# First modulation sums in four column groups, V's weights split on VectorE, the first unit packed in two halves

## The chip, the cores and the metric

The kernel runs on one core of a Trainium2 chip. The metric is the time of one execution on the device in microseconds (us), the median of several runs. Engines are named as the profile names them: PE is TensorE (its matmuls; PEld is its weight loads), DVE is VectorE, ACT is ScalarE, POOL is GpSimd, and SP is the engine that issues nearly all DMAs here; SPq stands for its queue.

## The reference

One transformer block with modulated norms, sequence 2048, width 576, 32 heads of 18, a causal window of 256 keys, and a mixer with an MLP of width 4608. All inputs are float32.

```
mod = (silu(c) @ w_mod).reshape(1, 6, 1, 576)
sa, ca, ga, sb, cb, gb = mod[:, 0], ..., mod[:, 5]
h = layernorm(x) * (1 + ca) + sa
x = x + ga * (windowed_attention(h @ wqkv) @ wo)
h = layernorm(x) * (1 + cb) + sb
x1 = h + shift(gelu(layernorm(h) @ w1)) @ w2
x = x + gb * (x1 + gelu(layernorm(x1) @ w3) @ w4)
```

The condition c is one row of 576 values, and w_mod is 576 x 3456. The change touches how `sa` and `ca` (the first 1152 columns of `w_mod`) are computed, and how the first quarter of the attention gets its operands.

## The kernel before

**Stages.** Phase A computes the norm, q, k and v, the attention and the output projection; phases B and C compute the mixer and the MLP. Sequence rows come in 16 tiles of 128; a group g is four tiles (512 rows). A unit is four heads of one group, so a group has 8 units, and attention has 32. The change is in phase A, in the work ahead of and around the first units of group 0.

**Precision.** Most products split each operand into a high half (a cast to fp32r) and a low half (the rest after subtraction), and sum three products: high by high, high by low, low by high. With 4 full row chunks and one of 64 rows this makes 14 matmuls for each item. So every weight and activation is first cast (mostly on ACT or POOL) and then subtracted (on DVE or POOL).

**Order.** Each piece of work is a small function with a hand-written time in units of an attention unit; `play` runs the pieces in the order of these times. That order is the order of instructions on each engine, and each engine works through its own list in order. Times below zero lie ahead of the first unit. So a piece that waits holds up all that stands behind it on its engine, SP's DMA issues included.

**The first stretch, in that order.** `warm` keeps PE busy with empty matmuls. `c_load` (L237) zeroes a tile, runs one Exp on ACT from that tile (which loads ACT's function table) and loads c. `wm_load` (L254) loads five row chunks of the needed part of `w_mod`. `cond` (L245) computes silu(c) and copies it to 128 equal columns for each chunk (`silub`). The four row tiles of group 0 are loaded and normalised (`x_norm`). `mod_sum(k)` (L269) multiplies a chunk of `w_mod` by the 128 equal columns, so that every partition of four PSUM banks holds the sums; `mod_col(j)` (L279) then picks out the diagonal of a 128x128 piece with the identity matrix as a mask, one DVE reduction for each piece of `sa` and `ca`, ten in all. `x_tr` (L357) transposes the normalised rows on PE, and then makes h on ACT with `sa` and `ca` (L373), its high half on POOL (L376) and its low half on DVE (L380), for five chunks.

**q, k and v of group 0.** `qk_item(g, c)` is one of nine blocks of 128 q or k features; blocks 0, 4 and 5 come first, as unit 0 needs rows of these. Its result is copied by ACT (L412), cast and subtracted by POOL (L416, L420), and stored by SP to arrays in device memory (`qd`, `kd`, L428 to L434). `v_item` is one half of a tile of V; V's weights are loaded by `v_load` (L322) and split by `v_split` (L326): cast on ACT (L330), subtracted on POOL (L334). `w_load` and `w_split` do the same for the blocks of q and k weights (L299, L306, L311). `kinds` and the table in the `v_item` loop name the PSUM bank each item uses: "mm" and "av" are single banks, "sc" is three and "st" two.

**The attention unit.** `pack(u)` (L457) reads the unit's q and k rows back from device memory into tiles with three copies (high, low and high of q; high, high and low of k), six transfers for Q (L467) and six for K (L469), in turn, all on SP. `scores(u)` multiplies them (L483), and a DVE reduction (L490) takes each row's maximum; the maxima go back into the Q tile by a DMA, and `attend(u)` computes the exponentials and the product with V (L530, L539, L549, L560). L560 writes the four heads of a unit to four groups of 32 output partitions.

**Tables that set the order.** `wt` (L664) has the times of the weight loads, `first` (L665) the times of the q/k items of group 0, `vt` (L689) those of the V items. Row buffers with the tag "r" are six; the tiles of x, `silub` and V's raw weights take them in turn. The tag "oT" has one buffer, not used yet this early.

## Time and profile before

| | |
|---|---|
| median of 3 runs | 1737.53 us (1730.81 to 1741.58) |
| profiled execution | 1739.16 us, span of the instructions 1737.4 us |
| mean granted PE clock | 0.989 |
| PE / PEld busy | 96% / 83% of the span |
| DVE / POOL / ACT busy | 67% / 47% / 40% |
| HBM traffic | 168.86 MB read, 111.78 MB written |

All times inside the execution count from the start of the span. A row of the timeline has the start, the time from the first to the last of the merged instructions, the engine, the line, the operation, what it writes and reads, the shape and the count; in brackets stands the idle time of the engine before it and what ended that. A row of a table by stretches has the stretch, its length, the busy time of PE, PEld, DVE, ACT and POOL with the number of instructions, the granted PE clock (1.00 is full), the busy share of the DMA engines and the GB/s. A row of a group has the busy time in us, the mean of one in ns, and the idle time before it with its releasers. PE's busy time counts each matmul from start to end, and matmuls overlap, so its start-to-start distance is read from rows with a count.

### The profile page before, as it was taken

What the parts mean: (1) busy time and instruction counts of PE and PEld (TensorE: products, weight loads), DVE (VectorE), ACT (ScalarE), POOL (GpSimd) and SP (SyncE); (2) the same over time, 40 slices, a digit from 0 to 9 for tenths busy, and PEclk for the clock granted to TensorE, in tenths of its full rate; (3) what the DMA queues carried; (4) which work ended last, traced back from release to release, by engine and by line L of the source; (5) the groups of instructions that cost most, each with busy time, mean ns of one, the idle gap of its engine ahead of it and who ended that gap; (6) DMA issues with size and microseconds to landing.
All of it is one profiled execution on the core that took longest, in us unless ns stands there. A gap on an engine that the chain in (4) does not pass through costs nothing.

```text
span 1737.4 us, 30750 instructions
## 1 busy us (share of the span) xinstructions
PE 1665.6 (96%) x11100; PEld 1439.1 (83%) x11100; DVE 1172.6 (67%) x2543; ACT 700.9 (40%) x1310; POOL 812.6 (47%) x799
## 2 busy tenths in 40 slices
PE   7899999999999889999999999999999999999997
PEld 5777777877777777788989999999998999999997
DVE  3465566665567574777778888888876666666667
ACT  3254464554455555443243444343422222222221
POOL 6433141332225453044178888888864333332335
PEclk9999999999999899999999999999999999999999
DMA  5735544534557563653456555556665554445441
GB/s 167 201 122 150 150 128 134 155 107 125 137 154 197 154 195 110 203 158 103 162 182 219 210 201 187 186 206 221 216 217 166 168 165 146 143 137 168 156 150 68
DMA packets 161279, 283.33 MB, mean 163 GB/s; under 512 B 38500, under 2 KB 77412, under 8 KB 161128
## 3 DMA queue, kind: packets, MB, share of 16 engines
q1 hardware_dynamic: 158184, 275.54, 50.8%
q10 hardware_dynamic: 2944, 5.83, 1.2%
q8 instruction: 88, 1.44, 0.4%
q14 instruction: 63, 0.52, 0.1%
HBM read 168.86 MB, written 111.78 MB: 162 GB/s over the span
## 4 chain that ended last, share of the span: by engine, by line
PE 81%; DMA 6%; DVE 5%; POOL 3%; ACT 2%; issue 1%; SPq 1%; ACTq 0%; POOLq 0%; DVEq 0%
PE pall L1283 26%; PE pall L1329 22%; PE pall L391 8%; PE pall L560 4%; PE pall L530 4%; PE pall L483 4%; PE pall L1017 3%; PE pall L539 3%; PE pall L1068 2%; PE pall L786 2%; DVE pall L490 1%; DMA Q<-ms 1%; DMA wm<-in_w_mod_dram 1%; PE pall L276 1%; PE pall L571 1%
## 5 line engine op out<-in xcount | busy, mean ns | idle before, releaser
L1283 PE MATMUL pall<-LNT,W 128*128 128x512 f32 x2016 | 498.5, 390 | 1.9 <-ACT g L1287 1.9
L1329 PEld LDWEIGHTS pall<-W,G 128*128 128x128 f32 x3036 | 430.0, 189 | 25.9 <-DVE G L1249 4.3
L1329 PE MATMUL pall<-W,G 128*128 128x288 f32 x3036 | 443.4, 295 | 5.7 <-DVE G L1249 3.6
L1283 PEld LDWEIGHTS pall<-LNT,W 128*128 128x128 f32 x2016 | 365.7, 188 | 61.6 <-ACT g L1287 2.2
L490 DVE CUSTOM_DVE_ANT_0 pall<-pall,mask 128x384 f32<-128x384 f32 (+2 forms) x512 | 271.0, 543 | 209.2 <-PE pall L483 205.8
L1338 DVE TENSOR_TENSOR accA<-pall,accA 128x576 f32<-128x576 f32 x336 | 254.2, 757 | 127.3 <-PE pall L1329 115.2
L1254 POOL TENSOR_TENSOR g<-g,g 128x512 f32<-128x512 f32 x140 | 183.9, 1314 | 293.5 <-DVE G L1249 151.1
L549 ACT ACTIVATE P<-pall 128x512 f32<-128x512 f32 (+2 forms) x384 | 215.3, 570 | 166.0 <-PE pall L539 149.5
L1246 ACT CAST G<-g 128x512 fp32r<-128x512 f32 x249 | 151.0, 620 | 282.0 <-POOL g L1254 280.3
L1249 DVE TENSOR_TENSOR G<-g,G 128x512 fp32r<-128x512 f32 x249 | 241.5, 971 | 4.1 <-ACT G L1246 4.1
L483 PE MATMUL pall<-K,Q 108*128 108x384 f32 (+2 forms) x512 | 188.4, 379 | 13.5 <-DMA xnd<-s4rows 4.0
L530 PE MATMUL pall<-Q,K 110*128 110x384 f32 (+1 forms) x704 | 156.8, 297 | 16.7 <-ACT P L549 12.4
L1287 ACT ACTIVATE g<-pall 128x512 f32<-128x512 f32 x144 | 85.8, 596 | 201.7 <-PE pall L1283 192.1
L391 PE MATMUL pall<-hT,Wc 128*128 128x512 f32 x504 | 159.2, 415 | 3.4 <-ACT V L454 1.9
L1338 DVE TENSOR_TENSOR accB<-pall,accB 128x576 f32<-128x576 f32 x134 | 101.4, 757 | 89.8 <-PE pall L1329 87.7
L530 PEld LDWEIGHTS pall<-Q,K 110*128 110x128 f32 x704 | 125.1, 192 | 39.1 <-ACT P L549 20.9
L416 POOL CAST qe<-qe 128x512 fp32r<-128x512 f32 x36 | 22.6, 627 | 240.8 <-ACT qe L412 230.4
L539 PE MATMUL pall<-maskb,identb 128*128 128x256 bf16 (+1 forms) x640 | 121.4, 255 | 0.0
L483 PEld LDWEIGHTS pall<-K,Q 108*128 108x128 f32 x512 | 97.5, 195 | 21.4 <-issue 8.8
L391 PEld LDWEIGHTS pall<-hT,Wc 128*128 128x128 f32 x504 | 86.1, 192 | 17.3 <-issue 3.9
L391 PE MATMUL pall<-Wv,hT 128*128 128x288 f32 x448 | 85.0, 313 | 3.5 <-POOL Wv L334 2.4
L560 PE MATMUL pall<-P,V 128*32 128x384 f32 (+2 forms) x1408 | 86.9, 394 | 0.0
(651 smaller groups left out, 2076.9 us busy)
## 6 DMA issues: line engine op xcount, KB each, us to landing
w4d<-W SPq DMA_DIRECT2D x55, 576.0 KB
W<-w4d SPq DMA_DIRECT2D x55, 576.0 KB
w3d<-W SPq DMA_DIRECT2D x36, 640.0 KB
W<-w3d SPq DMA_DIRECT2D x36, 640.0 KB
K<-k0d SPq DMA_DIRECT2D x96, 108.0 KB
r<-in_B_w_dram SPq DMA_DIRECT2D x36, 288.0 KB
Q<-q0d SPq DMA_DIRECT2D x128, 72.0 KB
K<-k1d SPq DMA_DIRECT2D x48, 108.0 KB
```

What stands on the lines that cost most here:

```text
L391: nc.tensor.matmul(pm, pl()[i][0], pl()[i][1], start=(i == 0), stop=(i == 13))
L483: nc.tensor.matmul(sc[:, lo:], q[0:2 * R3, h, i * P:(i + 1) * P], k[0:2 * R3, h // 2, i * P + lo:(i + 3) * P], start=True, stop=True)
L490: nc.vector.tensor_tensor_reduce(out=sc[:, lo:], in0=sc[:, lo:], in1=mask[:, lo:], scale=1.0, scalar=-3e38, op0=ALU.add, op1=ALU.max, accu ...
L530: nc.tensor.matmul(x[:, p0 * P:(p0 + w) * P], k[0:2 * R3 + 2, h // 2, (kb + 2) * P:(kb + 3) * P], q[0:2 * R3 + 2, h, q0 * P:(q0 + w) * P], ...
L539: nc.tensor.matmul(x[:, p0 * P:(p0 + w) * P], self.identb, m, start=False, stop=(n == len(ms) - 1))
L549: nc.scalar.activation(pt[:, c0:c1, h % 2, :], x[:, c0 * P:c1 * P].rearrange("p (a b) -> p a b", b=P), AF.Exp, scale=SCALE)
L560: nc.tensor.matmul(abox[0][32 * h:32 * h + 32, q0 * P:(q0 + w) * P], v[:, hh * VA:hh * VA + 32], Pt[b, h // 2][:, p0:p0 + w, h % 2, :], st ...
L1249: nc.vector.tensor_tensor(out=sp[m][:, 1], in0=src(), in1=sp[m][:, 0].bitcast(F32), op=sub)
L1254: nc.gpsimd.tensor_tensor(out=g[o] if o in g else gt(o), in0=g[a], in1=g[b], op=op)
L1283: nc.tensor.matmul(box["p"], box["l"][i][1], box["l"][i][0], start=(i == 0), stop=(i == 13))
L1329: nc.tensor.matmul(po, a, b, start=(n == 0), stop=(n == len(seq) - 1))
L1338: nc.vector.tensor_tensor(out=acc2[m, i], in0=po, in1=acc2[m, i], op=ALU.add)
```

## The change

Three things are done, and some times and bank names move with them.

**Modulation.** The equal columns are 32, not 128. The sums of a chunk are four matmuls with 320 columns each: shift and scale, columns 0 to 319 and 256 to 575. Each writes 32 output partitions of one bank. After the last chunk DVE copies the 128x320 result to SBUF (`mod_row`), PE transposes it in three pieces (`mod_tr`), and DVE picks one column of each group of 32 and adds 0 or 1 (`mod_col`, four instructions in place of ten reductions with their reads). The copy and `silub` share the buffer with the tag "oT", so `silub` no longer takes a row buffer. The table-loading Exp reads a constant, and only the unused corner of c's tile is zeroed, so that c's loads wait for neither.

**Splits.** The low halves of V's weights and of q/k block 0's weights go from POOL to DVE. V's splits get other times.

**Pack.** Unit 0's pack becomes two pieces: the Q transfers at -7.6, ahead of the load for block 6 and of block 5's stores, and the K transfers at -7.3 as before.

Besides: the weight load for block 1 goes behind V's loads; block 6's item is completed ahead of unit 0's scores (-1.08 to -0.98); several items take the other of the two banks; the last transpose of x takes a bank of "st".

```diff
-                nc.vector.memset(ct, 0.0)
-                nc.scalar.activation(silu[:, 0:1], ct[:, 0:1], AF.Exp)
+                nc.vector.memset(ct[TAIL:, KC:KC + 1], 0.0)
+                nc.scalar.activation(silu[:, 0:1], self.mhalf, AF.Exp)
...
-                wm["s"] = gp.tile([P, KC + 1, P], F32, tag="r", name="silub", bufs=6)
-                nc.vector.tensor_copy(wm["s"], silu.unsqueeze(2).to_broadcast([P, KC + 1, P]))
+                box = gp.tile([P, 480], F32, tag="oT", name="silub", bufs=1)
+                wm["s"], wm["r"] = box[:, 0:160].rearrange("p (k m) -> p k m", m=32), box[:, 160:480]
+                nc.vector.tensor_copy(wm["s"], silu.unsqueeze(2).to_broadcast([P, KC + 1, 32]))
...
             def mod_sum(k):
                 def f():
                     kk = P if k < KC else TAIL
-                    for v in range(2):
-                        for i, (c0, c1) in enumerate(half):
-                            if k == 0:
-                                wm[v, i] = ps([P, 512], ("sc", "st")[v], f"pms{v}{i}")
-                            nc.tensor.matmul(wm[v, i][:, 0:c1 - c0], wm["s"][:kk, k, :], wm["t"][:kk, k, v * D + c0:v * D + c1], start=(k == 0), stop=(k == KC))
+                    if k == 0:
+                        wm["p"] = ps([P, 320], "sc", "pms")
+                    for q, (v, c0) in enumerate((v, c0) for v in range(2) for c0 in (0, 2 * P)):
+                        nc.tensor.matmul(wm["p"][32 * q:32 * q + 32, :], wm["s"][:kk, k, :], wm["t"][:kk, k, v * D + c0:v * D + c0 + 320], start=(k == 0), stop=(k == KC))
                 return f
 
-            def mod_col(j):
...
-                        nc.vector.tensor_tensor_reduce(out=pm, in0=pm, in1=self.ident[:n, :n], scale=1.0, scalar=float(v), op0=ALU.mult, op1=ALU.add, accum_out=dst[:n, j:j + 1])
-                return f
+            def mod_row():
+                nc.vector.tensor_copy(wm["r"], wm["p"])
+
+            def mod_tr():
+                wm["q"] = ps([P, 3, P], "sc", "pmt")
+                for j in range(3):
+                    n = P if j < 2 else TAIL
+                    nc.tensor.transpose(wm["q"][:n, j, :], wm["r"][:, j * P:j * P + n], self.ident)
+
+            def mod_col():
+                for v, dst in ((0, sa), (1, ca)):
+                    pq = wm["q"].rearrange("p j (v i r) -> p v i j r", v=2, r=32)[:, v, :, :, 0]
+                    nc.vector.tensor_scalar(dst[:, 0:KC].rearrange("p (i j) -> p i j", j=2), pq[:, :, 0:2], float(v), None, op0=ALU.add)
+                    nc.vector.tensor_scalar(dst[:TAIL, KC:KC + 1], pq[:TAIL, 1, 2:3], float(v), None, op0=ALU.add)
...
-                    nc.gpsimd.tensor_tensor(out=w[:, l, :], in0=Wv["r", k], in1=w[:, h, :].bitcast(F32), op=ALU.subtract)
+                    nc.vector.tensor_tensor(out=w[:, l, :], in0=Wv["r", k], in1=w[:, h, :].bitcast(F32), op=ALU.subtract)
...
-            def pack(u):
+            def pack(u, qs=True, ks=True):
...
-                            nc.sync.dma_start(q[b + n * DH:b + n * DH + DH, hp::2, :].bitcast(F32), src)
+                            if qs:
+                                nc.sync.dma_start(q[b + n * DH:b + n * DH + DH, hp::2, :].bitcast(F32), src)
...
-            wt = {0: -8.975, 4: -8.974, 5: -8.973, 1: -8.972, 6: -7.45, ...}
-            first = {..., 6: (-1.06, -0.9), ...}
+            wt = {0: -8.975, 4: -8.974, 5: -8.973, 1: -8.7, 6: -7.45, ...}
+            first = {..., 6: (-1.08, -0.98), ...}
...
-            ev += [(-8.85 + 0.01 * j, mod_col(j)) for j in range(KC + 1)]
+            ev += [(-8.9, mod_row), (-8.89, mod_tr), (-8.885, mod_col)]
...
-            ev += w_split(0, -8.9, nc.gpsimd.tensor_tensor) + ...
+            ev += w_split(0, -8.9, nc.vector.tensor_tensor) + ...
...
-                ev += v_split(k, -7.9 + 0.05 * k)
+                ev += v_split(k, -7.98 + 0.07 * k)
...
-            kinds = {0: "mm", 4: "av", 5: "mm", 1: "mm", 6: "mm"}
+            kinds = {0: "mm", 4: "av", 5: "mm", 1: "av", 6: "mm", 2: "av"}
...
-                ev += put(v_item(n // 2, n % 2, {0: "av", 1: "mm", 2: "av", 3: "mm", 4: "av"}.get(n, "mm")), t0, t0 + 0.2)
+                ev += put(v_item(n // 2, n % 2, {0: "av", 3: "av", 4: "av", 7: "av"}.get(n, "mm")), t0, t0 + 0.2)
...
-                ev.append((u - self.o_p if u > 1 else (-7.3, -1.5)[u], pack(u)))
+                if u == 0:
+                    ev += [(-7.6, pack(0, ks=False)), (-7.3, pack(0, qs=False))]
+                else:
+                    ev.append((u - self.o_p if u > 1 else -1.5, pack(u)))
```

More of the change, by code (lines that the diff above doesn't have):

```diff
@@ L265, in warm @@
                 return f
-            half = ((0, 2 * P), (2 * P, D))
             def mod_sum(k):
@@ L363, in tr @@
                         hT[g] = gp.tile([P, 2 * KC + 1, 512], F32R, tag="L", name=f"hT{g}", bufs=1)
-                    pa = box["p"] = ps([P, 4, P], ("tr", "mm", "tr", "mm", "tr")[k] if g else ("mm", "tr", "av", "sc", "tr")[k], f"hT{g}_{k}")
+                    pa = box["p"] = ps([P, 4, P], ("tr", "mm", "tr", "mm", "tr")[k] if g else ("mm", "tr", "av", "sc", "st")[k], f"hT{g}_{k}")
                     for i in range(4):
@@ L663, in phase_a @@
             order = [0, 4, 5, 1, 6, 2, 7, 3, 8]
-            wt = {0: -8.975, 4: -8.974, 5: -8.973, 1: -8.972, 6: -7.45, 2: -1.9, 7: -1.5, 3: -1.2, 8: -0.9}
-            first = {0: (-8.2, -8.0), 4: (-7.95, -7.75), 5: (-7.7, -7.5), 1: (-2.08, -1.75), 6: (-1.06, -0.9), 2: (0.05, 0.4), 7: (0.9, 1.2), 3: (1.35, 1.65), 8: (1.8, 2.1)}
-            ev = [(-9.5, warm(24)), (-9.45, consts), (-9.44, vones(0, 4)), (-9.4, c_load), (-9.2, wm_load), (-9.05, cond)]
+            wt = {0: -8.975, 4: -8.974, 5: -8.973, 1: -8.7, 6: -7.45, 2: -1.9, 7: -1.5, 3: -1.2, 8: -0.9}
+            first = {0: (-8.2, -8.0), 4: (-7.95, -7.75), 5: (-7.7, -7.5), 1: (-2.08, -1.75), 6: (-1.08, -0.98), 2: (0.05, 0.4), 7: (0.9, 1.2), 3: (1.35, 1.65), 8: (1.8, 2.1)}
+            ev = [(-9.5, warm(24)), (-9.45, consts), (-9.44, vones(0, 4)), (-9.405, c_load), (-9.2, wm_load), (-9.05, cond)]
             ev += [(-7.4, lambda: clear(1)), (-7.35, lambda: clear(2)), (-1.2, vones(4, 10))]
@@ L674, in phase_a @@
             ev += [(wt[c], w_load(c)) for c in order]
-            ev += w_split(0, -8.9, nc.gpsimd.tensor_tensor) + w_split(4, -8.3, nc.vector.tensor_tensor) + w_split(5, -8.1, nc.vector.tensor_tensor)
+            ev += w_split(0, -8.9, nc.vector.tensor_tensor) + w_split(4, -8.3, nc.vector.tensor_tensor) + w_split(5, -8.1, nc.vector.tensor_tensor)
             for c in order[3:]:
```

9 lines of the change are left out of this document (2 added, 7 removed).

## The prediction

> **What bounds the kernel now.** First the page's busy shares, then the same by stage, because a mean hides the start.
>
> ```profile
> span 1737.4 us, 30750 instructions
> PE 1665.6 (96%) x11100; PEld 1439.1 (83%) x11100; DVE 1172.6 (67%) x2543; ACT 700.9 (40%) x1310; POOL 812.6 (47%) x799
> ```
>
> ```profile
> core 0: us, PE busy (x) PEld busy (x) DVE busy (x) ACT busy (x) POOL busy (x), PEclk, DMA share, GB/s
> 0.00:25.00 25.00, 20.98 (x80) 13.06 (x80) 7.48 (x27) 4.25 (x7) 12.90 (x31) 0.93 0.75 218
> 25.00:39.00 14.00, 11.59 (x50) 8.17 (x49) 7.80 (x27) 9.03 (x16) 10.15 (x10) 1.00 0.38 123
> 39.00:51.00 12.00, 9.08 (x43) 7.80 (x42) 1.88 (x2) 2.11 (x5) 11.81 (x10) 0.86 0.47 132
> 51.00:70.00 19.00, 15.82 (x87) 13.43 (x85) 7.68 (x33) 4.20 (x10) 9.02 (x12) 0.91 0.77 182
> ...
> 110.00:200.00 90.00, 88.36 (x687) 68.21 (x689) 51.57 (x191) 43.66 (x89) 26.58 (x28) 1.00 0.49 135
> ```
>
> From 110 us PE is 98% busy: what follows the start moves with it. The change edits only work before about 76 us. There PE stands idle some 4.0 + 2.4 + 2.9 + 3.2 us (stretch less PE busy) and runs below full clock in three of four stretches; POOL fills 39 to 51 us while DVE does almost nothing. The timeline gives the chain:
>
> ```profile
> 2.24 0.39 SPq L242 DMA_DIRECT2D ct<-in_c_dram  x1
> ...
> 4.83 2.48 SPq L258 DMA_DIRECT2D wm<-in_w_mod_dram  x5
> ...
> 11.75 7.75 PE L276 MATMUL pall<-wm,silub 128*128 128x256 f32 x24 [3.14 <-DMA wm<-in_w_mod_dram]
> ...
> 13.17 0.58 DVE L160 TENSOR_SCALAR x<-x,a3mv,a3rs 128x576 f32<-128x576 f32 x1 [0.97 <-POOL a3rs L138]
> ...
> 19.25 0.62 ACT L306 CAST Wc<-wr 128x512 fp32r<-128x512 f32 x1 [6.15 <-DMA wr<-in_A_wqkv_dram]
> 19.34 1.91 PE L366 MATMUL pall<-ident,x 128*128 128x128 f32 x16
> ...
> 21.09 4.24 PE L276 MATMUL pall<-wm,silub 128*128 128x256 f32 x16
> ...
> 25.22 2.79 ACT L373 ACTIVATE h<-pall,sa,ca 128x512 f32<-128x512 f32 x4 [5.14 <-DVE ca L286]
> ...
> 31.09 0.68 DVE L380 TENSOR_TENSOR hT<-h,hT 64x512 fp32r<-64x512 f32 x1 [0.51 <-POOL hT L376]
> ...
> 35.32 5.58 POOL L334 TENSOR_TENSOR Wv<-wvr,Wv 128x576 fp32r<-128x576 f32 x4
> ...
> 38.79 1.48 PE L391 MATMUL pall<-Wv,hT 128*128 128x288 f32 x10
> ...
> 40.17 1.27 DVE L311 TENSOR_TENSOR Wc<-wr,Wc 128x512 fp32r<-128x512 f32 x1 [6.67 <-ACT Wc L306]
> 40.84 1.07 POOL L416 CAST qe<-qe 128x512 fp32r<-128x512 f32 x1
> ...
> 41.94 0.49 SPq L428 DMA_DIRECT2D q0d<-qe  x1
> ...
> 43.37 3.71 PE L391 MATMUL pall<-Wv,hT 128*128 128x288 f32 x15 [1.75 <-POOL Wv L334]
> ...
> 46.40 0.53 SPq L299 DMA_DIRECT2D wr<-in_A_wqkv_dram  x1
> ...
> 47.57 3.47 PE L391 MATMUL pall<-hT,Wc 128*128 128x512 f32 x14 [0.49 <-ACT V L454]
> ...
> 50.87 3.86 PE L391 MATMUL pall<-Wv,hT 128*128 128x288 f32 x28
> ```
>
> Read it in this order. The modulation sums hold PE from 11.75 to 25.3 us (with the 1.91 us of transposes between) and with them the first h on ACT at 25.22. The last low half of h ends at 31.8; q and k items follow. Then POOL makes V's low halves while V's matmuls wait for them and while the casts of the second q/k item (40.84) queue behind them. What that costs is seen where the first unit's scores begin:
>
> ```profile
> 48.25 0.53 SPq L432 DMA_DIRECT2D k0d<-qe  x1
> ...
> 54.96 0.27 SPq L469 DMA_DIRECT2D K<-k1d  x1
> ...
> 59.96 0.30 PE L483 MATMUL pall<-K,Q 108*128 108x128 f32 x1 [2.60 <-DMA K<-k1d]
> ...
> 60.68 0.51 SPq L467 DMA_DIRECT2D Q<-q0d  x1
> ...
> 62.93 0.30 DVE L490 CUSTOM_DVE_ANT_0 pall<-pall,mask 128x128 f32<-128x128 f32 x1 [2.28 <-PE pall L483]
> ...
> 66.04 0.32 SPq L469 DMA_DIRECT2D K<-k1d  x1
> ...
> 71.01 0.30 PE L483 MATMUL pall<-K,Q 108*128 108x128 f32 x1 [0.90 <-DMA wr<-in_A_wqkv_dram]
> ```
>
> 59.96 is unit 0's first score, released by the last K transfer of its pack; 71.01 is unit 1's, released by its own pack. I forecast these two.
>
> **The modulation.** Its 40 records cost 7.75 + 4.24 = 12 us. Column groups are not shown for this product, but the attention's products use four of them:
>
> ```profile
> 94.59 2.15 PE L560 MATMUL pall<-P,V 128*32 128x384 f32 x32
> ```
>
> These are four heads over 9 x 128 = 1152 columns (key blocks against 3, 1, 3 and 2 query tiles in unit 0): 1.8 ns per column for all four, so 320 columns cost 0.6 us and five chunks 2.9. The other end, no overlap at all, is the present rate times 320/288: about 13. I take 2.9, from the same form. The c load no longer waits for ACT's first activation (2.24 becomes about 1.15), so the modulation weights go out at 3.7, not 4.83, and land near 10.5. But the row norms hang on POOL and still end at 13.75, so the 16 transposes run to about 15.7 and the last two chunks to 16.9. Added are a 128x320 copy out of PSUM, three transposes (0.12 each by the 16 in 1.91) and four small picks on DVE:
>
> ```profile
> L490 DVE CUSTOM_DVE_ANT_0 pall<-pall,mask 128x384 f32<-128x384 f32 x8 | 4.3, 585 | 0.5 <-PE pall L483 0.4
> ...
> L248 DVE TENSOR_SCALAR silu<-silu 128x5 f32<-128x5 f32 x1 | 0.6, 568 | 4.5 <-ACT silu L247 4.5
> ```
>
> The copy lies between the 0.3 of a 128x128 reduction (62.93, below) and this 0.59; I take 0.5. A pick lies between nothing and 0.57, four between 0 and 2.3; I take 0.25 each. Modulation is ready near 18.9 with the handovers. Next late is ACT's queue: the cast of the first weights stands ahead of the first h, and these land at 19.25, or up to 1.1 earlier with the modulation weights ahead of them; plus 0.9 (19.25 and the quarter after it) that is 19.1 to 20.2. First h: **20.2 for 25.22, a lead of 5.0** (0 if unoverlapped, 6 at best).
>
> From there to the last low half took 31.77 - 25.22 = 6.5 us. Ten reductions leave DVE, but the first weights' low half (0.97 from the 512 and 128 forms) comes to it ahead of them, beside ACT's first h; POOL's casts set the rate. I keep 6.2 to 6.5. Item 0 then ends near 27.1, and two more at 3.3 each bring PE to V at 33.7 (38.8 before).
>
> ```profile
> L311 DVE TENSOR_TENSOR Wc<-wr,Wc 128x512 fp32r<-128x512 f32 x5 | 4.0, 805 | 16.9 <-ACT Wc L306 16.9
> ```
>
> **V's low halves.** POOL loses five of 1.4 (5.58 for four): 7 us. DVE gains five: 0.9 each by the mean of L311 scaled 576/512, up to 1.43 by its slowest (the 1.27 at 40.17, beside a POOL cast); 4.5 to 7.1 us in a stretch where DVE is idle. V's loads come earlier too: two row buffers are free at once, and the second-last weight load stands behind them. So V's first two items cost 3.86 (the row at 50.87) and not the 8.3 from 38.79 to 47.08 (43.37 + 3.71): 4.4 us. The new bank kinds take three waits of about 0.49 on V's evacuation. PE then runs V, V, item 1, V, V and all of item 6: 33.7 + 3.9 + 3.5 + 3.9 + 3.5 = 48.5.
>
> Against this stands a rule. The Trainium skill (SBUF — State Buffer, Terms, "shared port pair") says that VectorE and GpSimd take one port pair by exclusive lock and the loser blocks for the whole instruction. The 1.27 at 40.17, against a mean of 0.8, agrees. By the rule POOL's casts could slip by another 2 us, and the sum would be 10 rather than 12.
>
> **The pack.** Item 4 reaches ACT near 30.4, POOL casts and subtracts by 33, its stores (4.4 us of SP from 41.94 to 46.40, with the wait for the subtraction; 3.8 without) end near 35.6. Then the six Q transfers, each 0.36 apart, to 38; the load for item 6 (46.40 to 48.25, 1.8) to 39.8; item 5's stores, 2.0, to 41.8; the six K transfers with a wait of up to 1 us on the stores just issued, to 44.6. The last took 59.96 - 54.96 = 5.0 to be usable; with half as many in flight 2.5 to 4.7: 47.1 to 49.3. Unit 0's scores thus begin near **48.5**, K and PE arriving together. Queued behind Q on SP are the item 6 load and item 5's stores; PE needs the former at about 45; issued by 39.8, with a landing like the pack's it is there at 44.8 at the latest, and its split (0.9 and 1) can cost PE 1 us.
>
> **What is late next.** DVE's reductions run from 62.93 until unit 1's first score, 8.1 us, so that score could begin near 57. Its pack cannot: SP first issues a weight load (1.8), item 1's stores, another load, and then the pack, as long as before (66.36 - 60.68 = 5.7), to 54.6; landing took 4.6. Item 1's halves come from POOL behind the clears of the other Q and K buffers:
>
> ```profile
> L216 POOL MEMSET Q<- 128x2048 f32 x3 | 5.4, 1809 | 0.1
> L217 POOL MEMSET K<- 32x1536 f32 x3 | 4.1, 1376 | 0.2
> ```
>
> Two of each are 6.4 us, from 36 to 42.4, then the halves to 44.4, in time for SP. Unit 1's first score: **59.2 for 71.01: 11.8 us**. Beyond I take nothing; two more bank waits of 0.5 might go, and up to 3 us be lost again. The profiled execution took 1739.2 (span 1737.4 and 1.8 around it): 1727. The median, 1737.5, stands 1.7 below: **1726**.
>
> **Rivals.** *Half clock* (0.20): PE's clock fell to half after each longer idle.
>
> ```profile
> 13.00:14.00 1.00, 1.00 (x4) 0.73 (x3) 0.58 (x1) 0.10 (x1) 0.13 (x1) 0.50 1.11 332
> ```
>
> With 9 us less PE work before 25 us, PE idles more there; two or three half-rate stretches of 3.3 us cost 1.6 each: 3 to 5, a gain of 7 to 9, 1728.5 to 1730.5. The Trainium skill (TensorE: Matmul & The Clock Gate, Part 1) says the same: an idle window of about 3.4 us halves the clock. *More* (0.12): K and unit 1's pack land in 2.5 us, so DVE sets 57.3 and bank waits go too: 14.5 to 17, 1720.5 to 1723. *The edit is idle* (0.06): column groups do not overlap, or the gain returns in a later transfer wait; 0 to 5, 1732.5 to 1737.5. *Slower* (0.04): the clock stays halved through the whole start. PE has some 37 us of work before 59 us; at half rate as much again is added, and the lead is gone from about 12 us of added time, a slowdown of up to 20: 1738 to 1757. The returns to full clock at 16 and 47 us speak against it.
>
> **Chances.** My forecast, a gain of 10 to 14, holds 0.58. The range 1715 to 1735 leaves out the slower case, most of the idle one and the noise beyond (the three times shown span 10.8). About 1%, or 17 us, is what a measurement here can tell from no change; only *more*, helped by that spread, reaches it: faster 0.13, same 0.83, slower 0.04.
>
> **What would show it.** The 40 records of L276's successor end before 18 us, first h near 20; V's low halves on DVE and no V matmul waiting for them; unit 0's first score at 47 to 50, unit 1's at 57 to 60; the stretch from 110 us on unchanged in length. Wrong would be: a half-clock row in 16 to 30, first h after 22, PE waiting for item 6's weights, or the lead at 71 us shrinking afterwards.

## The result and the profile after

The changed kernel takes 1728.4 us, the median of 8 runs (1724.39 to 1734.67), against 1738.16 for the kernel before in the same session (8 runs, 1730.81 to 1742.5). The gain is 9.8 us by the medians. The ratio is 0.9951 with a 95% interval of 0.993 to 0.9972, by which the gain is 8.5 us. Either way it is half a per cent, less than the 1% that the prediction took as the bound of a change. The forecast was 1726.

The profiled execution took 1724.57 us. That is one of the shortest of the eight, while the profiled execution of before (1739.16) lies a little above its median, so the two profiles differ by 14.6 us and overstate the gain. The text comes back to why.

By the page's busy shares little has changed: PE is busy for 96% of the span as before, DVE for 68% and not 67%. The table has the same stretches as in the prediction, with one long stretch behind them. The columns are those of the table by stretches above.

```profile
0.00:25.00 25.00, 18.54 (x93) 8.80 (x94) 10.14 (x34) 7.48 (x12) 14.54 (x33) 0.85 0.90 252
25.00:39.00 14.00, 14.00 (x69) 11.95 (x69) 11.51 (x14) 7.89 (x17) 9.69 (x8) 0.90 0.43 118
39.00:51.00 12.00, 10.81 (x60) 9.15 (x58) 2.06 (x11) 2.69 (x6) 11.60 (x14) 1.00 0.74 231
51.00:70.00 19.00, 15.05 (x74) 12.90 (x73) 10.31 (x44) 3.18 (x8) 2.16 (x3) 0.82 0.63 166
...
400.00:800.00 400.00, 365.95 (x2899) 304.04 (x2899) 260.43 (x814) 199.62 (x374) 149.12 (x181) 0.99 0.55 157
```

The same long stretch before:

```profile
400.00:800.00 400.00, 367.26 (x2868) 303.70 (x2867) 254.61 (x807) 201.65 (x373) 140.03 (x170) 0.97 0.55 155
```

DVE does 11.51 us of work in 25 to 39 us where it did 7.80, and DMA is busier in 39 to 51 us (0.74 against 0.47): V's low halves and unit 0's pack have come there. The clock column is the other half of the story. Up to 70 us the time lost to a clock under full is, each stretch times the share that its clock lacks, 3.8 + 1.4 + 0 + 3.4 = 8.6 us; before it was 1.8 + 0 + 1.7 + 1.7 = 5.2. (These are upper estimates, since half clock costs nothing where PE stands idle.) From 400 to 800 us it is the other way round: 4 us after, 12 before.

The timeline of the changed kernel has the rows that answer those in the prediction:

```profile
1.18 0.42 SPq L242 DMA_DIRECT2D ct<-in_c_dram  x1
...
11.54 2.73 PE L274 MATMUL pall<-wm,silub 128*32 128x320 f32 x16 [0.54 <-DMA wm<-in_w_mod_dram]
...
14.20 3.58 PE L369 MATMUL pall<-ident,x 128*128 128x128 f32 x16
...
17.70 1.42 PE L274 MATMUL pall<-wm,silub 128*32 128x320 f32 x16
...
18.00 0.62 ACT L309 CAST Wc<-wr 128x512 fp32r<-128x512 f32 x1 [4.89 <-DMA wr<-in_A_wqkv_dram]
...
19.19 0.49 DVE L278 COPY silub<-pall 128x320 f32<-128x320 f32 x1 [5.45 <-PE pall L274]
...
20.71 2.78 ACT L376 ACTIVATE h<-pall,sa,ca 128x512 f32<-128x512 f32 x4 [1.89 <-DVE ca L290]
...
26.58 0.68 DVE L383 TENSOR_TENSOR hT<-h,hT 64x512 fp32r<-64x512 f32 x1 [0.50 <-POOL hT L379]
...
29.58 6.04 DVE L337 TENSOR_TENSOR Wv<-wvr,Wv 128x576 fp32r<-128x576 f32 x5 [0.59 <-ACT Wv L333]
...
29.73 1.76 POOL L423 TENSOR_TENSOR qe<-qe 128x512 fp32r<-128x512 f32 x1
...
32.23 1.01 POOL L419 CAST qe<-qe 128x512 fp32r<-128x512 f32 x1 [0.74 <-ACT qe L415]
...
34.56 3.87 PE L394 MATMUL pall<-Wv,hT 128*128 128x288 f32 x28
...
37.01 0.55 SPq L471 DMA_DIRECT2D Q<-q0d  x1
...
39.19 0.32 SPq L471 DMA_DIRECT2D Q<-q0d  x1
...
45.59 0.27 SPq L474 DMA_DIRECT2D K<-k1d  x1
...
49.50 0.54 PE L488 MATMUL pall<-K,Q 108*128 108x128 f32 x3 [0.98 <-DMA wr<-in_A_wqkv_dram]
...
50.94 0.51 SPq L471 DMA_DIRECT2D Q<-q0d  x1
...
61.64 0.30 PE L488 MATMUL pall<-K,Q 108*128 108x128 f32 x1 [2.90 <-DMA wr<-in_A_wqkv_dram]
```

The reader is to see four things. The first h starts at 20.71 (25.22 before). V's first 28 matmuls run in one row of 3.87 us and wait for nothing. Unit 0's scores start at 49.50 (59.96) and unit 1's at 61.64 (71.01). And PE's idle time of 2.90 us ahead of unit 1's score has grown: before it was 0.90. The view puts this wait down to a weight load on SP's queue, before as after; a score reads only K and Q, so I take it as the wait for the unit's pack, which went out on the same queue just ahead.

How early the later units are is read from the instruction that negates a unit's maxima on DVE. For units 1 and 31 it starts, before and after, at:

```profile
87.49 0.17 DVE L496 TENSOR_SCALAR mr<-m 128x16 fp32r<-128x16 f32 x1
...
674.35 0.17 DVE L496 TENSOR_SCALAR mr<-m 128x16 fp32r<-128x16 f32 x1
```

```profile
79.27 0.17 DVE L501 TENSOR_SCALAR mr<-m 128x16 fp32r<-128x16 f32 x1
...
660.32 0.17 DVE L501 TENSOR_SCALAR mr<-m 128x16 fp32r<-128x16 f32 x1
```

The lead is 8.2 us at unit 1 and 14.0 at unit 31. Between them it stands still over many units (8.1 to 8.2 from unit 2 to 7, 9.3 from 9 to 18) and then moves in steps, most of them up. So the start that the change edits gave 8.2 us in this pair of profiles. The rest came where nothing was edited, and most of it fits the half clock of 400 to 800 us, 12 us before and 4 after.

### The profile page after: what moved, and what is told of

It is laid out like the page before. It is cut to its first block, busy times and chain, and to the rows that moved or that the text cites. A ratio compares the mean times of both kernels' runs of the same rounds, so it can differ in the third digit from the quotient of the medians.

```text
span 1722.8 us, 30741 instructions
## 1 busy us (share of the span) xinstructions
PE 1652.6 (96%) x11103; PEld 1429.4 (83%) x11103; DVE 1177.1 (68%) x2535; ACT 700.1 (41%) x1310; POOL 804.9 (47%) x792
## 4 chain that ended last, share of the span: by engine, by line
PE 81%; DMA 6%; DVE 5%; ACT 2%; POOL 2%; SPq 1%; issue 1%; ACTq 0%; POOLq 0%; DVEq 0%
PE pall L1291 26%; PE pall L1337 23%; PE pall L394 9%; PE pall L565 4%; PE pall L535 4%; PE pall L488 4%; PE pall L544 2%; PE pall L1025 2%; PE pall L1076 2%; PE pall L794 2%; DMA xp<-s4rows 1%; DVE pall L495 1%; DMA wm<-in_w_mod_dram 1%; DMA s4rows<-od 1%; DMA Q<-ms 1%
## 5 line engine op out<-in xcount | busy, mean ns | idle before, releaser
L1291 PEld LDWEIGHTS pall<-LNT,W 128*128 128x128 f32 x2016 | 365.5, 188 | 61.8 <-ACT g L1295 2.2
```

The costliest lines, as they stand in the source:

```text
L1291: nc.tensor.matmul(box["p"], box["l"][i][1], box["l"][i][0], start=(i == 0), stop=(i == 13))
```

## The experiments

Lead means the time by which unit 1's maxima are negated earlier than before (87.49). Less half clock is the mean time minus the mean of (1 - granted clock) x span, an estimate of the time that the same run would have at a full clock throughout. The clock is known to 0.001, which is 1.7 us in one run. The kernel before has 1739.1, a clock of 0.9886 and 1719.3 by this (mean of 67 runs). In the two rows with a star block 6 of k is left out, as said below.

| kernel | median us (runs) | ratio, 95% interval | lead | mean clock | less half clock |
|---|---|---|---|---|---|
| changed | 1728.4 (8) | 0.9951 (0.993 to 0.9972) | 8.2 | 0.9885 | 1708.8 |
| changed, again | 1731.22 (6) | 0.9951 (0.9935 to 0.9968) | 9.9 | 0.9867 | 1707.9 |
| old sums | 1733.07 (5) | 0.9963 (0.995 to 0.9975) | 6.8 | 0.9884 | 1712.8 |
| V on POOL | 1738.05 (11) | 1.0000 (0.9986 to 1.0015) | 2.5 | 0.9854 | 1712.8 |
| pack in one piece | 1730.58 (5) | 0.9958 (0.9943 to 0.9974) | 10.5 | 0.9860 | 1707.9 |
| V on DVE alone | 1735.66 (10) | 0.9967 (0.9951 to 0.9983) | 6.8 | 0.9891 | 1716.0 |
| more empty matmuls at the start | 1731.78 (1) | | 10.5 | 0.986 | 1707.6 |
| block 7's load behind the pack | 1730.3 (6) | 0.9949 (0.9926 to 0.9972) | 13.4 | 0.9862 | 1706.4 |
| loads issued by ACT | 1734.69 (12) | 0.9971 (0.9954 to 0.9988) | 6.2 | 0.9859 | 1710.4 |
| PE's gaps filled * | 1729.69 (11) | 0.9943 (0.9924 to 0.9962) | 9.6 | 0.9884 | 1709.0 |
| all of these * | 1722.49 (6) | 0.991 (0.9882 to 0.9937) | 14.4 | 0.9902 | 1706.3 |
| all, in order | 1723.27 (5) | 0.9901 (0.9883 to 0.992) | 14.1 | 0.9912 | 1707.9 |
| all but the filled gaps | 1724.74 (5) | 0.9913 (0.9897 to 0.9929) | 13.4 | 0.9898 | 1707.8 |

Each ratio is against the kernel before in the same session. Ratios compare; medians of different sessions do not, quite. The lead is that of one profile each; the changed kernel, unedited, has 8.2 and 9.9.

### The changed kernel again, and the old sums

The first run repeats the changed kernel unedited. The second has its V splits, pack and tables, but the modulation of before: 20 full-width sums over 128 equal columns and the reductions with the mask (`silub` with 128 columns lies in the "oT" buffer, and the last transpose of x has its old bank):

```diff
-                    for q, (v, c0) in enumerate((v, c0) for v in range(2) for c0 in (0, 2 * P)):
-                        nc.tensor.matmul(wm["p"][32 * q:32 * q + 32, :], ...
+                    for v in range(2):
+                        for i, (c0, c1) in enumerate(half):
...
+                            nc.tensor.matmul(wm[v, i][:, 0:c1 - c0], wm["s"][:kk, k, :], ...
-            ev += [(-8.9, mod_row), (-8.89, mod_tr), (-8.885, mod_col)]
+            ev += [(-8.85 + 0.01 * j, mod_col(j)) for j in range(KC + 1)]
```

> The changed kernel as it is, as the measure for the three runs beside it. Both theories: first h near 20.7 us, V's first matmul near 34.6, unit 0's first score near 49.5, unit 1's near 61.6, and a time 7 to 12 us below the kernel before (ratio 0.993 to 0.996).

> The changed kernel with the old modulation sums (20 full-width products, ten diagonal reductions); c's early load, the splits and the pack stay changed. Theory (a chain, each lead is handed on): first h at 24 to 24.5 instead of 20.7, unit 0's first score at 52.5 to 53.5 and unit 1's near 65, the time 3 to 4 us above the changed kernel. Rival (SP's stream of transfers sets the start, the sums are hidden under it): first h as late, but unit 0's and unit 1's first scores within 1 us of 49.5 and 61.6, and the time within 1.5 us of the changed kernel.

The changed kernel gave the same ratio, 0.9951, in another session. The timeline has the first h of its repeated profile and, in the second fence, the sums and the first h of the kernel with the old sums:

```profile
19.45 2.79 ACT L376 ACTIVATE h<-pall,sa,ca 128x512 f32<-128x512 f32 x4 [1.02 <-DVE ca L290]
```

```profile
10.58 6.06 PE L276 MATMUL pall<-wm,silub 128*128 128x256 f32 x24 [1.97 <-DVE a2st L131]
...
22.35 0.78 ACT L373 ACTIVATE h<-pall,sa,ca 128x512 f32<-128x512 f32 x1 [3.28 <-DVE ca L286]
```

With the old sums the first h is at 22.35, so only 1.6 to 2.9 us of the lead at this point are the column groups' own (20.71 and 19.45). The other 2.9 (25.22 to 22.35) are mostly not the change's at all. The kernel of the next section with V on DVE alone has the old sums and also the old, late load of c, and its first h is at 22.63: there the sums begin at 10.86 and 24 of them take 6.06 us, where the profile of before has 11.75 and 7.75, with a clock of 0.50 from 13 to 15 us. So 2.6 us of the 4.5 by which the first h came earlier are a slow start of the one execution that was profiled before, and the earlier load of c is worth some 0.3 us here. The granted clock is 1.00 over 0 to 25 us with the old sums and 0.85 with the new ones.

The lead is handed on: unit 0's first score is at 50.86 and unit 1's at 62.66, 1.4 and 1.0 us behind the first profile of the changed kernel, 2.8 and 2.8 behind the repeated one (48.09 and 59.84). By the prices of the expectation it would have been more, as the first h was forecast at 24. In time, the sums are worth 0.0012 of the ratio, some 2 us, which their intervals hardly tell from nothing; less half clock the difference is 1712.8 - 1708.4 (the mean of the two rows above it) = 4.4.

### V's low halves

One run has the changed kernel with V's low halves back on POOL, another has the kernel before with V's low halves on DVE and nothing else. In both it is one line:

```diff
-                    nc.vector.tensor_tensor(out=w[:, l, :], in0=Wv["r", k], in1=w[:, h, :].bitcast(F32), op=ALU.subtract)
+                    nc.gpsimd.tensor_tensor(out=w[:, l, :], in0=Wv["r", k], in1=w[:, h, :].bitcast(F32), op=ALU.subtract)
```

> The changed kernel with V's low halves back on POOL, at the changed times. Theory: POOL's five subtractions of 1.4 us stand ahead of item 4's cast, which moves from 32.2 to 36 to 37; V's first matmul waits; unit 0's first score at 53.5 to 55, unit 1's at 65 to 67, the time 4 to 5 us above the changed kernel. Rival (V's split is worth only the waits of V's matmuls, which the pack hides): unit 0's first score within 1.5 us of 49.5, the time within 1.5 us of the changed kernel.

> The kernel before with one edit: V's low halves on DVE. Theory (POOL's queue was late for the pack as well as for V): first h stays at 25.2, item 4's cast comes at 36 to 37 instead of 40.84, unit 0's first score at 53.5 to 55 instead of 59.96, unit 1's at 65 to 66 instead of 71.01, the time 4 to 6 us below the kernel before. Rival (the split only counts once the modulation is short): both scores within 1.5 us of before and the time within 1.5 us.

With V back on POOL nothing of the gain was left: a ratio of 1.0000. The timeline of that kernel:

```profile
32.76 4.19 POOL L337 TENSOR_TENSOR Wv<-wvr,Wv 128x576 fp32r<-128x576 f32 x3
...
36.87 1.10 POOL L419 CAST qe<-qe 128x512 fp32r<-128x512 f32 x1
...
39.42 2.26 PE L394 MATMUL pall<-Wv,hT 128*128 128x288 f32 x15 [1.75 <-POOL Wv L337]
...
54.29 0.54 PE L488 MATMUL pall<-K,Q 108*128 108x128 f32 x3 [1.30 <-DMA K<-k1d]
```

V's matmuls wait for POOL again, and item 4's cast stands behind POOL's subtractions: 36.87 and not 32.23, 4.6 us, and unit 0's scores come 4.8 us later (54.29 for 49.50). That is the chain the prediction drew. In time the line is worth more than the 4 to 5 us expected: 1738.05 against 1731.22 for the changed kernel of the same session, 6.8 us. So V's subtraction is the part of the change without which the others gain no time.

Where the rest went is seen in the clock. PE idles where it waits for POOL (11.79 us busy of 14 in 25 to 39 us), and the stretch around the first scores has 0.79 where the profile of before has 0.91:

```profile
51.00:70.00 19.00, 13.50 (x64) 11.29 (x63) 9.14 (x40) 2.10 (x5) 5.70 (x9) 0.79 0.79 201
```

From 70 to 110 us it is 0.93 against 1.00. Unit 0's maxima still come 6.9 us earlier than before, unit 1's 2.5, and unit 3's 0.3 later. Over all runs of the session this kernel loses 25.4 us to half clock and the one before 18.8: less half clock it is 6.5 us below (1719.3 - 1712.8), but its mean clock of 0.9854 is the lowest of the table. That PE's waits are what lowers the clock is argued here; the run with the gaps filled bears on it.

Alone on the old kernel the edit gains 0.0033 of the ratio, 3.0 to 8.5 us by its interval. Its first scores:

```profile
52.41 0.30 PE L483 MATMUL pall<-K,Q 108*128 108x128 f32 x1 [2.04 <-DMA wr<-in_A_wqkv_dram]
```

They come 7.6 us earlier than before (59.96), more than was expected, but 2.6 of these are the first h at 22.63, which the edit does not touch. From the first h to item 4's cast it takes 11.3 us (33.91 - 22.63) in place of 15.6 (40.84 - 25.22): the edit's own 4.3 us.

One side of it had a price. Beside the five subtractions on DVE, POOL's own subtraction took 1.76 us; alone it took 1.27, as the row of before shows:

```profile
43.28 1.27 POOL L420 TENSOR_TENSOR qe<-qe 128x512 fp32r<-128x512 f32 x1
```

The next, at 33.33, took 1.68. Two such rows cost POOL 0.9 us together, and DVE's took 6.04 / 5 = 1.2 us each, in the middle of 0.9 to 1.43. The Trainium skill (SBUF — State Buffer, Terms, "shared port pair") says that VectorE and GpSimd take one port pair by exclusive lock and the loser blocks for the whole instruction. The rows agree in direction, but POOL's grew by 0.4 to 0.5 us beside instructions of 1.2, and together by half of the 2 us that the prediction worked out from the rule.

### The pack in one piece

```diff
-                    ev += [(-7.6, pack(0, ks=False)), (-7.3, pack(0, qs=False))]
+                    ev.append((-7.3, pack(0)))
```

> The changed kernel with unit 0's pack in one piece at -7.3. Theory: SP issues without a gap from item 4's stores to the last K transfer, so the last K transfer still goes out near 45.6 and only its landing suffers from twelve instead of six transfers in flight: unit 0's first score at 49.5 to 51, unit 1's near 61.6 to 62.5, the time within 1.5 us of the changed kernel. Rival (the halves take six issues, 2.2 to 2.6 us, off the path): unit 0's first score 2 to 3 us later, near 52, and the time 2 to 3 us above.

The ratio is 0.9958, the changed kernel's 0.9951, with intervals that overlap. SP issues nearly without a pause from 33 to 45 us in both, with the last transfer at 44.74 here and 45.59 there. Here all twelve go out in one run, and PE waits longer for unit 0 (2.23 us against 0.98), but unit 1's score starts no later:

```profile
49.96 0.53 PE L488 MATMUL pall<-K,Q 108*128 108x128 f32 x3 [2.23 <-DMA q0d<-qe]
...
60.26 0.30 PE L488 MATMUL pall<-K,Q 108*128 108x128 f32 x1 [1.27 <-DVE mr L501]
```

The split of the pack is worth nothing that these runs can tell.

### More empty matmuls at the start

```diff
-            ev = [(-9.5, warm(24)), ...
+            ev = [(-9.5, warm(34)), ...
```

> The changed kernel with 34 empty matmuls at the start instead of 24, so that PE works until the first sums can start. Theory (the first h waits for sums and transposes at half clock): granted clock 1.00 in 12.2 to 15.6 us, the 16 transposes in 2.3 us or less instead of 2.3 to 3.6, first h at 18.8 to 19.5. Rival (first h waits for the first weights' cast, whatever the clock): first h at 19.5 or later although the clock is 1.00.

The timeline of PE in that run:

```profile
12.90 0.74 PE L274 MATMUL pall<-wm,silub 128*32 128x320 f32 x8 [0.69 <-DMA wm<-in_w_mod_dram]
13.58 1.97 PE L369 MATMUL pall<-ident,x 128*128 128x128 f32 x16
...
19.14 2.78 ACT L376 ACTIVATE h<-pall,sa,ca 128x512 f32<-128x512 f32 x4 [0.62 <-DVE ca L290]
```

and a stretch of its table:

```profile
20.00:25.00 5.00, 4.35 (x10) 3.03 (x11) 3.38 (x4) 3.94 (x8) 4.47 (x5) 0.50 0.95 299
```

PE goes from the empty matmuls into the sums at 10.88 us, the clock stays at 1.00 until 19 us, the 16 transposes take 1.97 us where they took 3.58, and the first h comes at 19.14 instead of 20.71. A chunk of sums is 0.74 us at a full clock. So the theory holds for the first h. But the half clock comes right behind it, 0.50 over 20 to 25 us, and unit 0's first score, at 48.42, is no earlier than in the repeated run of the unedited kernel (48.09). The one time there is, 1731.78 at a clock of 0.986, lies among those of the unedited kernel; one run can't show more.

### Block 7's load behind unit 1's pack, and loads issued by ACT

```diff
-            wt = {..., 7: -1.5, 3: -1.2, 8: -0.9}
+            wt = {..., 7: -1.45, 3: -1.2, 8: -0.9}
```

> The changed kernel with the weight load of item 7 issued behind unit 1's pack instead of ahead of it. Theory (SP's issues ahead of unit 1's pack set unit 1's start): unit 0's first score unmoved (48 to 49.5), unit 1's 9.8 to 10.6 us behind it instead of 11.8 to 12.1, the time 1 to 2 us below the changed kernel. Rival (landing or DVE sets it): the distance stays at 11.5 or more and the time is unmoved.

The move takes three issues (49.25 to 50.9 us in the changed kernel) from the front of unit 1's pack. The timeline of this kernel:

```profile
49.25 0.39 SPq L471 DMA_DIRECT2D Q<-q0d  x1
...
58.33 0.30 PE L488 MATMUL pall<-K,Q 108*128 108x128 f32 x1 [0.82 <-DMA wr<-in_A_wqkv_dram]
```

The pack starts at 49.25 and not at 50.94, and unit 1's score at 58.33, after a wait of 0.82 us and not 2.90. That is 8.5 us behind unit 0's score at 49.80 (12.1 in the changed kernel), less than the 9.8 to 10.6 expected: the place of the wait was right. The lead is 13.4. Yet the 1 to 2 us of time did not come: the ratio is 0.9949, the same as that of the changed kernel.

The second run leaves SP only what the attention needs: the weight loads of blocks 6, 2, 7, 3 and 8 are issued by ACT.

```diff
-                    nc.sync.dma_start(raws[c][:, 0:KC, :], ...
+                    eng = nc.sync if c in (0, 4, 5, 1) else nc.scalar
+                    eng.dma_start(raws[c][:, 0:KC, :], ...
```

> The changed kernel with the weight loads of items 6, 2, 7, 3 and 8 issued by ACT, not SP, at the same times in the order. Theory (as for the run before): SP reaches unit 0's K transfers 1.7 us sooner and unit 1's pack 5 us sooner; unit 0's first score at 47 to 48.5, set by PE, unit 1's 8.5 to 9.5 us behind it, set by DVE's reductions, the time 2 to 4 us below the changed kernel. Rival (ACT's issues delay its copies and exponentials, or more transfers in flight land later): unit 1's distance stays above 11 or the time is no lower.

At 0.9971 this gains less than the changed kernel, though the intervals overlap. The timeline shows ACT's loads and SP's pack side by side:

```profile
38.23 0.50 SPq L473 DMA_DIRECT2D Q<-q0d  x1
...
39.69 0.39 ACTq L303 DMA_DIRECT2D wr<-in_A_wqkv_dram  x1
...
44.12 0.27 SPq L473 DMA_DIRECT2D Q<-q0d  x1
...
51.39 0.27 SPq L476 DMA_DIRECT2D K<-k1d  x1
...
55.27 2.40 PE L490 MATMUL pall<-K,Q 108*128 108x128 f32 x7 [5.56 <-DMA q0d<-qe]
```

The Q transfers, six in 2.5 us before (37.01 to 39.5), now take from 38.23 to 44.4, the last of the K transfers goes out at 51.39 and not at 45.59, and PE waits 5.56 us for unit 0. (0.9 us of this delay is the run's later first h, at 21.57.) In SP's single order the large loads stood behind the small transfers that are needed at once. Whether it is the shared DMA engines or a slot for issues that delays SP's rows was not tried.

### PE's gaps filled

Where did the 5 us of the moved load go? The two profiles by stretches, first the changed kernel, then the one with the load moved:

```profile
48.00:51.00 3.00, 1.81 (x9) 1.08 (x7) 1.17 (x9) 0.59 (x1) 2.92 (x6) 1.00 0.90 273
...
52.00:55.00 3.00, 3.00 (x14) 3.00 (x13) 1.18 (x6) 0.00 (x0) 0.00 (x0) 0.50 0.51 137
...
58.00:61.00 3.00, 0.67 (x2) 0.19 (x1) 2.14 (x10) 0.27 (x1) 0.00 (x0) 1.00 0.93 160
```

```profile
52.00:55.00 3.00, 3.00 (x22) 2.85 (x22) 2.41 (x11) 1.10 (x3) 0.19 (x1) 1.00 0.53 158
```

Behind its idle times at 48.5 and 58.7 us the changed kernel runs some 3.4 us at a clock of 0.50: 14 matmuls in 52 to 55 us, where the other kernel does 22; 62 to 65 us are at 0.50 too. Each such stretch costs 1.7 us, and the first steps up in the changed kernel's lead over the later units (1.2, 1.7 and 1.9 us) have about this size. It is not the luck of one execution: the six profiles with unit 1's pack and PE's gaps as in the changed kernel (both of its own, the old sums, V on POOL, the pack in one piece, more empty matmuls) have 0.79 to 0.84 over 51 to 70 us, the one with the load moved has 1.00. The next run fills the gaps with empty matmuls:

```diff
-            ev = [(-9.5, warm(24)), ... (-9.05, cond)]
+            ev = [(-9.5, warm(24)), ... (-9.05, cond), (-0.975, warm(3)), (-0.81, warm(2)), (0.0, warm(8))]
```

The first three write into the bank that holds block 6's sums before ACT has copied them, so k's block 6 comes out as zeros in this kernel and in the first of the next section; the instructions and their order are those of the full work.

> The changed kernel with 13 empty matmuls (128x512, bf16) put where PE stands idle: three ahead of unit 0's first score, two among its scores, eight ahead of unit 1's first score. In the changed kernel's profile the granted clock is half from 51.8 to 55.2 and from 61.8 to 65.3 us, behind PE's idle time at 48.5 to 50 and 58.8 to 61.6. Theory A, the half-rate stretches follow PE's idle time: both are gone, the granted clock is 1.00 from 50 to 66 us, the lead at unit 1's maxima rises from the 8 to 10 us of the changed kernel to 11.5 to 13.5, and if nothing is given back later the time falls by about 3 us, to 1725 to 1727. Theory B, the clock falls at its own times whatever PE does: half-rate stretches of 3.3 us stay in 50 to 66, the lead stays at 8 to 10, the time within 1 us of 1729. Theory C, the stretches go but as many come back in the later attention units: the lead rises as in A, and the time is still 1728 to 1731.

```profile
51.00:70.00 19.00, 16.19 (x98) 12.91 (x99) 12.28 (x54) 4.49 (x10) 3.60 (x4) 1.00 0.63 188
70.00:110.00 40.00, 37.32 (x278) 28.95 (x278) 26.19 (x102) 23.72 (x47) 11.06 (x17) 0.96 0.47 150
```

Both stretches of half clock are gone (1.00 over 51 to 70 us, 0.82 before the edit), as theory A said. The lead at unit 1 is 9.6, less than A's 11.5: this run's first h came 0.9 us later than the changed kernel's, and its scores wait for the same transfers. A half-clock stretch lies behind 70 us (0.96 up to 110 us; the changed kernel has 1.00 there, and 0.96 in its repeated profile), the lead is 8.0 at unit 3, and the ratio, 0.9943, is that of the changed kernel. For the mechanism A holds, for the time C.

### A version that beats both

The load moved, 34 empty matmuls at the start, and the gaps filled; then the same with the first three empty matmuls behind the copy of block 6's item; then the same without the seven empty ones around the scores. The second one's edit:

```diff
-            ev = [(-9.5, warm(24)), ... (-9.05, cond)]
+            ev = [(-9.5, warm(34)), ... (-9.05, cond), (-0.9695, warm(3)), (-0.81, warm(2)), (0.0, warm(2))]
-            wt = {..., 7: -1.5, 3: -1.2, 8: -0.9}
+            wt = {..., 7: -1.45, 3: -1.2, 8: -0.9}
```

> The changed kernel with everything that gave an earlier start: the weight load of block 7 behind unit 1's pack, 34 empty matmuls at the start instead of 24, and empty matmuls ahead of the first scores (three, two and two). Theory A: no half-rate stretch from 8 to 66 us but around the modulation's transposes, first h near 19.3, unit 0's first score near 48.5, unit 1's near 57, a lead of 14 to 15 at unit 1's maxima, and a time of 1722 to 1726, below both kernels. Theory B: half-rate stretches stay in 50 to 66, a lead near 12, 1727 to 1730. Theory C, what is gained at the start is given back as half-rate time later: a lead of 14 at unit 1's maxima and a time of 1728 to 1731.

> The changed kernel with the load of block 7 behind unit 1's pack, 34 empty matmuls at the start, and three, two and two empty ones around unit 0's first scores and ahead of unit 1's; the first three stand behind the copy of block 6's item, whose bank they use, and so wait about 0.5 us for ACT. Theory A (an earlier start and less half-rate time add up): 1.00 granted from 51 to 70 us, unit 1's first score near 57.5, a lead of 12 to 14.5 at unit 1's maxima, a time of 1721 to 1725 and a ratio of 0.990 to 0.993. Theory C (what the start gains comes back as half-rate time in later units): the same lead at unit 1, and 1727 to 1731, a ratio of 0.994 to 0.996.

> As the run before, without the seven empty matmuls around the first scores: only the load of block 7 behind unit 1's pack and 34 empty matmuls at the start. By the profile of the run with the load moved alone, PE had no half-rate stretch from 48 to 76 us even without them, since its idle times there were 0.9 us each. If the empty matmuls do nothing beyond the clock, this one has the same lead at unit 1 (12 to 14.5) and the same time, 1721 to 1725. If the empty matmuls themselves are what keeps the clock up, half-rate stretches of 3.3 us come back in 48 to 66 us, the lead is 9 to 11 and the time 1726 to 1731.

All three have a lower ratio than the changed kernel: 0.991, 0.9901 and 0.9913. The intervals of the second and third end at 0.992 and 0.9929, below the 0.993 at which the changed kernel's begins, for the third by a hair; that of the first, which leaves out block 6 of k, ends at 0.9937 and overlaps. The second one's profile by stretches:

```profile
51.00:70.00 19.00, 17.73 (x120) 15.27 (x118) 13.86 (x54) 6.58 (x14) 1.90 (x2) 1.00 0.78 199
70.00:110.00 40.00, 37.24 (x283) 28.41 (x281) 28.58 (x111) 25.10 (x50) 13.04 (x19) 1.00 0.47 146
```

Neither stretch is below full clock, and the lead is 14.1 at unit 1 and 15.0 at unit 16. The seven empty matmuls around the scores are worth at most a microsecond or two (0.9901 against 0.9913, intervals that overlap); without them one half-clock stretch came back (0.91 over 51 to 70 us). What the moved load did not do alone, and the 34 empty matmuls not in their one run, they did together: 0.004 to 0.005 of the ratio, 7 to 9 us. By the last two columns of the table the changed kernel has 1707.9 to 1708.8 less half clock and loses 20 to 23 us to it, and the three versions have 1706.3 to 1707.9 and lose 15 to 18. So most of their gain is a clock that stays up. Where in the 1720 us it stays up is not shown: beyond 110 us the second one's profile, at 0.992 over all, is hardly different from the changed kernel's at 0.991.

## Why the prediction was right, and where it was not

The forecast of 1726 stands 2.4 us from the measured 1728.4, which lies inside the range, and the change is within 1%, as expected. The gain is another matter: 9.8 us by the medians and 8.5 by the ratio, below the 10 to 14 that I gave 0.58, and the rival *half clock* had 7 to 9 and 1728.5 to 1730.5. Step by step:

- **First h at 20.2.** Measured 20.71, and 19.45 and 19.75 in the repeated run and the one with the whole pack. The number holds by luck, the way to it does not. The forecast let ACT's cast of the first weights decide; those landed early (cast at 18.00), and the modulation itself was last. Its terms: five chunks of sums at 0.74 us are 3.7, not 2.9; the copy took 0.49 for 0.5; the four picks 0.36 together for 1.0. The term that was missing is the clock: two of the five chunks and the transposes ran at 0.50, and the sums ended at 19.1 and not at 16.9. The price of the old sums was also read from rows at half clock: 24 of them are 6.06 us, not 7.75, and the 25.22 that the lead of 5.0 counts from was itself late by 2.6 against the other profile of the same lines.
- **Last low half 6.2 to 6.5 us behind.** 26.58 + 0.68 - 20.71 = 6.55. V's first matmul came at 34.56 for 33.7.
- **V's low halves.** 1.2 us each, inside 0.9 to 1.43; no V matmul waits; V and V take 3.87 for 3.86. V's matmuls were to gain 4.4 us; with the line taken away unit 0's scores are 4.8 us later.
- **Unit 0's score at 48.5.** 49.50, and 48.09 in the repeated run. The last K transfer went out at 45.59, a microsecond or so behind the forecast's chain. The first h (0.5) and POOL's slower subtractions (0.9) more than account for that. That the weights of block 6 are there by 44.8 was right: PE starts that item at 45.16 without a wait.
- **Unit 1's score at 59.2, a lead of 11.8.** This step failed in the profile: 61.64, a lead of 9.4, and 8.2 at its maxima. The pack set the score, as forecast: its issues took 6.3 us for 5.7 and landed in 4.4 for 4.6, but they started at 50.94 and not 48.9. SP's chain ahead of them was mis-sized by 2 us, of which 1.3 were handed on from unit 0's pack (its last issue ended at 45.9 and not at 44.6). Between the score and the maxima another 1.2 us of the lead went, which fits the half clock of 61.8 to 65.3; the sum had nothing for the clock. The rival *half clock*, two or three stretches of 1.6 us and a gain of 7 to 9, describes the first 90 us of this profile better than the forecast does; I gave it 0.20.
- **Beyond, nothing.** The lead did change there, from 8.1 to 14.0 us, in steps. That PE is 98% busy from 110 us on was read from 110 to 200 us; from 400 to 800 it is busy for 367 of 400 us before and 366 after, so what follows the start need not simply move with it. In the profile this looks like a gain of 14.6. Less half clock the changed kernel is 10.5 to 11.4 us faster than before (1719.3 against 1708.8 and 1707.9), near the 12 of the sum, and in the time 9.8 and 7.3 arrived, by the medians of the two sessions.
- **The pack in halves** was given no price of its own, but the sum let K land in time because half as many transfers would be in flight. The run in one piece shows that this made no difference to the time.

Of the signs of being wrong, the half clock in 16 to 30 us was there (0.85 over 0 to 25 us, 0.90 over 25 to 39), and so was the shrinking lead. The time came out near the forecast partly by luck: the lead was counted from a profile with a slow start, and the sum left out half clock, which over all runs costs the changed kernel 19.9 us, and 23.1 in the repeat, against 19.8 for the kernel before. The order of block 1's load, block 0's low halves on DVE and the bank names were not tried alone, so what they are worth is open.

## What to carry to other kernels

Removing PE work ahead of a stage that waits leaves PE idle, and half clock behind the idle time can cost as much as the work did, as with V on POOL here: look at the granted clock of the stretch behind each new gap. Price old work from rows at full clock, and take the starting point from more than one profile. Of several edits to one chain, find the one without which the others gain nothing; here it was a line that moves five subtractions from the engine that everybody waited for. Moving large loads to another engine's queue is not free either: here the last of the small transfers that the first scores need went out 5.8 us later.

## What the hardware showed that was not expected

Runs of the changed kernel differ by up to 10 us, and nearly all of that is the granted clock. Its first eight runs, each with its clock and the time less half clock:

```
us           1724.39 1724.57 1724.73 1727.19 1729.61 1731.34 1732.88 1734.67
clock        0.992   0.991   0.990   0.989   0.988   0.987   0.986   0.985
less half    1710.6  1709.1  1707.5  1708.2  1708.9  1708.9  1708.6  1708.7
```

The second row falls as the first rises, and the third stays within 3.1 us. For the kernel before the clock explains less: its 67 runs span 14.9 us, and 9.6 less half clock. It follows that a comparison of two single profiles of this kernel can be wrong by 10 us where the work is the same.

The Trainium skill (TensorE: Matmul & The Clock Gate, Part 1) says that the clock is halved after an idle window of about 3.4 us. The length of the stretches agrees (51.8 to 55.2 us), and there are some of twice that length (10.7 to 17.5 us in the changed kernel). But the window need not be wholly idle: in 48 to 51 us PE was busy for 1.81 of 3.00 us ahead of such a stretch, with no idle time longer than 0.98 us, and in the kernel with the load moved for 1.87 of 3.00 with none behind it:

```profile
48.00:51.00 3.00, 1.87 (x9) 1.19 (x8) 0.86 (x7) 0.59 (x1) 2.92 (x7) 1.00 0.93 288
```

Nor is there one in the changed kernel behind an idle microsecond at 67.8 us. What decides between the two was not settled. Nor was why time saved at the start so often came back as half clock in later units: the run with the filled gaps shows that it did, and the versions that combine the edits show that it need not.
